# Attention and two MoE layers on one core: the first pass in a computed, pinned order with one PSUM pool, and a second pass that is all Strassen with weight blocks split beforehand

## The chip, the cores and the metric

One core of one Trainium2 chip. The number is the device time of one execution in microseconds; kernels are compared by the median of several runs. All matrix work runs on TensorE (PE; PEld is its weight load), the element-wise work on VectorE (DVE), ScalarE (ACT) and GpSimd (POOL), and SyncE (SP) issues nearly all DMAs.

## The reference

Attention over 4 batches of 8 heads (S = 576, D = 64) with a causal local part and a memory part, then two feed-forward layers over the 2304 tokens (d_model 512):

```
a = softmax(causal(q @ k.T / sqrt(D))); local = a @ v
q_p = elu(q) + 1
mem_out = (q_p @ M_prev) / (q_p . z_prev + 1e-6)
x = g * mem_out + (1 - g) * local            # g = sigmoid(beta), per head
x = (silu(x @ w_gate) * (x @ w_val)) @ w_out # d_ff 1536
h = x @ w_in                                 # d_ff 2048
out = (h * sigmoid(1.702 * h)) @ w_out
```

The weights arrive as float64 and are turned into float32 on the chip.

## The kernel before, in words

**Arithmetic.** A float32 product is made of three matmuls in the fp32r type: each operand is split into a high part (a cast on ACT) and a low part (a subtraction, operand minus high part), and PE sums high x high, low x high and high x low. One matmul is a 128x128 weight block against 288 columns; two of them fill one PSUM tile of two banks (288 + 288 columns, 576 tokens of one batch).

**Weights.** They come in 68 chunks of 128x512: per group of the first layer (3 groups) 8 projection chunks (gate and value) and 4 output chunks, per group of the second layer (4 groups) 4 and 4. The chain of one chunk is: load (SP, tile w), two ACT operations (L140, L141), three on DVE (L144, L146, L147), one add on POOL (L150), which leaves the float32 chunk in a tile wa (three buffers); then the split, hi on ACT (L166) and lo on POOL (L169), into wp (four buffers). Of the 20 pairs of projection chunks POOL also forms four Strassen sums (L178 to L181); these and the chunks themselves go to DRAM as float32. The 28 output chunks go to DRAM split.

**Stages.** (1) The attention of batches 0 and 1 alone: 8 pairs (two heads of one batch each), in an order that `ordered` computes and `pinned` fixes on every engine; it ends with three chunks of weights made. (2) The first pass: both layers for batches 0 and 1 (`moe`: per chunk and batch h, 12 x 2 matmuls, tile m), with the attention of batches 2 and 3 between them: `beside` lists its steps with hand-set costs, and the loop over `moe(xh, xl)` issues them as the pass proceeds, so much attention per half product. The order on an engine is that of the program text. The finished attention goes to DRAM (`stage`). PSUM is split: two tiles for MoE (ps_m) and two for attention (ps_s). (3) The second pass (`second`): both layers for batches 2 and 3. A projection pair is one Strassen unit (`unit`): 7 products of 12 matmuls (tile wb against sums of x, L82) in place of 8, with PSUM results added on DVE into tiles sn; the weight sums are read raw (7 of 128x256 in one load, L730) and split on the spot (ACT L742, POOL L743). The output blocks are plain: 28 chunks x 2 batches x 24 matmuls. The gate is Tanh on ACT with a multiply-add on DVE behind it (L836, L837).

Between the passes, SP loads the attention of batches 2 and 3 back (xr, L966), and `halves` forms the Strassen operands of x: B11, B12, B21, B22 and T1 to T4, each split.

## Time and profile before

| | us |
|---|---|
| median of 3 runs | 1081.33 (1080.96 to 1081.98) |
| profiled execution | 1082.06 |
| its span in the trace | 1080.3 |
| PE busy | 1041.8 (96%) |
| PE's weight load busy | 971.8 (90%) |
| DVE busy | 696.1 (64%) |
| POOL busy | 612.3 (57%) |
| ACT busy | 542.9 (50%) |

Times are read from one profiled execution. An engine is busy while an instruction of it runs; "idle before" a group is the time in which its engine stood still just before, and the arrow names what it waited for. Names such as m, wp, sn are the program's tiles. PEclk is the share of full clock that PE was granted.

### The profile page before, as it was taken

Reading aid. Unit: us, or ns where it says so; the run is one execution under the profiler, and the core shown is the slowest. Engines: PE = TensorE matmul, PEld = TensorE weight load, DVE = VectorE, ACT = ScalarE, POOL = GpSimd, SP = SyncE. Lnnn points to the kernel's source line nnn. Section 1 sums busy time; section 2 is a strip of 40 time slices with the busy share of each in tenths; the row PEclk is TensorE's granted clock in tenths of the full one; section 3 lists DMA queues with packets and bytes.
Section 4 is the critical chain, followed back from the end, with each engine's and each line's share of the span. In section 5 each row is a group of like instructions: output and inputs, shape, how many; then the busy total and the mean of one; then the engine's idle time right before and its main releaser. Section 6 shows DMA issues by size and latency. Waiting matters only on the chain.

```text
span 1080.3 us, 19843 instructions
## 1 busy us (share of the span) xinstructions
PE 1041.8 (96%) x7664; PEld 971.8 (90%) x7664; DVE 696.1 (64%) x1063; ACT 542.9 (50%) x1107; POOL 612.3 (57%) x634
## 2 busy tenths in 40 slices
PE   5989798999999999999999999999999999999998
PEld 2656687899999898989899999999999999999998
DVE  6887589646666777836657448762745778265573
ACT  4887555655545555756556454442513436343230
POOL 6886798866567475665745542661835817153321
PEclk8999999999999999999999999999999999999999
DMA  4332635644454453444434337323222222322102
GB/s 165 114 95 87 216 118 187 219 148 146 151 170 142 132 174 123 157 137 147 161 122 140 115 127 278 110 71 110 70 79 87 85 78 70 112 74 74 59 21 88
DMA packets 46718, 133.93 MB, mean 124 GB/s; under 512 B 7584, under 2 KB 10400, under 8 KB 46624
## 3 DMA queue, kind: packets, MB, share of 16 engines
q1 hardware_dynamic: 46480, 132.67, 36.7%
q8 instruction: 60, 0.98, 0.4%
q14 instruction: 34, 0.28, 0.1%
q10 hardware_dynamic: 144, 0.00, 0.0%
HBM read 92.54 MB, written 40.11 MB: 123 GB/s over the span
## 4 chain that ended last, share of the span: by engine, by line
PE 54%; DVE 3%; ACT 1%; DMA 1%; POOL 1%; issue 1%; SPq 0%; ACTq 0%; DVEq 0%; POOLq 0%
PE m L82 51%; PE o L82 1%; PE s L82 1%; DVE hl L613 1%; PE tp L378 1%; DMA xr<-x 0%; DMA raw<-w 0%; DVE u L683 0%; ACT hh L612 0%; ACT wb L742 0%; POOL wa L150 0%; DVE xl L766 0%; DMA x<-st 0%; DVE wa L147 0%; POOL p L366 0%
## 5 line engine op out<-in xcount | busy, mean ns | idle before, releaser
L82 PE MATMUL m<-hh,wp 128*128 128x288 f32 x1792 | 312.6, 297 | 1.4 <-ACT acc L663 0.7
L82 PEld LDWEIGHTS m<-hh,wp 128*128 128x128 f32 x1792 | 262.2, 189 | 9.5 <-issue 3.2
L82 PE MATMUL m<-xh,wp 128*128 128x288 f32 x1280 | 241.8, 304 | 12.6 <-DVE u L643 8.9
L743 POOL TENSOR_TENSOR wb<-raw,wb 128x256 fp32r<-128x256 f32 x140 | 124.9, 906 | 197.4 <-ACT wb L742 192.3
L82 PEld LDWEIGHTS m<-xh,wp 128*128 128x128 f32 x1280 | 193.9, 191 | 23.8 <-DVE u L643 8.1
L82 PE MATMUL m<-hl,wp 128*128 128x288 f32 x896 | 190.6, 296 | 0.0
L150 POOL TENSOR_TENSOR wa<-wa,wr 128x512 uint32<-128x512 uint32 x68 | 93.6, 1377 | 106.3 <-issue 50.2
L82 PEld LDWEIGHTS m<-hl,wp 128*128 128x128 f32 x896 | 143.6, 188 | 0.4 <-issue 0.4
L82 PE MATMUL m<-xl,wp 128*128 128x288 f32 x640 | 138.2, 298 | 0.0
L82 PE MATMUL m<-xh,wb 128*128 128x288 f32 x640 | 119.0, 296 | 0.0
L169 POOL TENSOR_TENSOR wp<-wa,wp 128x512 fp32r<-128x512 f32 x68 | 92.7, 1364 | 42.5 <-ACT wp L166 42.1
L82 PEld LDWEIGHTS m<-xl,wp 128*128 128x128 f32 x640 | 104.4, 191 | 0.0
L82 PEld LDWEIGHTS m<-xh,wb 128*128 128x128 f32 x640 | 96.9, 189 | 0.0
L742 ACT CAST wb<-raw 128x256 fp32r<-128x256 f32 x140 | 55.6, 404 | 79.1 <-PE m L82 77.6
L366 POOL TENSOR_SCALAR p<-p,sm 128x128 f32<-128x128 f32 (+3 forms) x128 | 75.1, 605 | 28.6 <-DVE sm L357 8.5
L82 PE MATMUL m<-th,wb 128*128 128x288 f32 x480 | 90.3, 296 | 0.0
L144 DVE TENSOR_SCALAR wa<-wa 128x512 f32<-128x512 f32 x68 | 39.3, 578 | 75.6 <-ACT wa L140 75.0
L341 ACT ACTIVATE p<-s,nm 128x128 f32<-128x128 f32 (+3 forms) x128 | 66.0, 528 | 30.5 <-DVE nm L327 29.3
L82 PEld LDWEIGHTS m<-th,wb 128*128 128x128 f32 x480 | 73.2, 189 | 0.0
L140 ACT ACTIVATE wa<-w 128x512 f32<-128x512 f32 x68 | 46.0, 677 | 53.5 <-POOL wp L169 48.9
L613 DVE TENSOR_TENSOR hl<-u,hh 128x576 fp32r<-128x576 f32 x56 | 56.4, 1007 | 25.4 <-ACT hh L612 24.6
L141 ACT ACTIVATE wr<-w 128x512 uint32<-128x512 uint16 x68 | 46.1, 678 | 51.0 <-POOL wa L150 50.4
(136 smaller groups left out, 1830.6 us busy)
## 6 DMA issues: line engine op xcount, KB each, us to landing
w<-w SPq DMA_DIRECT2D x40, 512.0 KB, 3.7
raw<-w SPq DMA_DIRECT2D x20, 896.0 KB, 4.6
w<-wo SPq DMA_DIRECT2D x28, 512.0 KB, 3.6
w<-wp SPq DMA_DIRECT2D x28, 512.0 KB, 2.9
wp<-w SPq DMA_DIRECT2D x28, 512.0 KB, 3.5
w<-sums SPq DMA_DIRECT2D x20, 512.0 KB, 2.8
qk<-qk SPq DMA_DIRECT2D x32, 288.0 KB, 3.7
nq<-nat SPq DMA_DIRECT2D x16, 320.0 KB, 4.1
```

The costliest lines, as they stand in the source:

```text
L82: nc.tensor.matmul(o, w, x, start=start, stop=stop)
L140: nc.scalar.activation(a, top.bitcast(F32), AF.Abs)
L141: nc.scalar.activation(r, rest, AF.Copy, scale=2.0 ** -13)
L144: nc.vector.tensor_scalar(a, a, HIGH, LOW, op0=ALU.min, op1=ALU.max)
L150: nc.gpsimd.tensor_tensor(au, au, r, op=ALU.add)
L169: nc.gpsimd.tensor_sub(wp[:, 1], t, f(wp[:, 0]))
L341: nc.scalar.activation(p[:, j, c:c + n], s[:, j, c:c + n], AF.Exp, bias=nm[:, x, j:j + 1], accum_out=sm[:, x, j:j + 1])
L366: nc.gpsimd.tensor_scalar(p[:, j, c:c + n], p[:, j, c:c + n], sm[:, x, j:j + 1], 1.0, op0=ALU.mult, op1=ALU.mult)
L378: nc.tensor.transpose(t[:, j, c:c + 128], p[:, j, c:c + 128], ident)
L613: nc.vector.tensor_sub(hl, t, f(hh))
L742: nc.scalar.copy(wb[:, 0], src)
L743: nc.gpsimd.tensor_sub(wb[:, 1], src, f(wb[:, 0]))
```

## The change

- **First pass.** `beside`, `alone` and `moe` are replaced by lists of operations: `attend` (attention pairs), `piece` (one weight chunk: load, decode, split, store, sums) and `first_pass` (the MoE products, in halves of 12 matmuls, and what follows them). Each operation has an engine, a cost, a key (when it is due), what it comes after, and what it takes and gives back of counted stocks (buffers). `ordered` runs them through a list schedule, and `pinned` fixes the result on every engine, as for the first stage.
- **PSUM.** One pool of four tiles (psp) serves attention and MoE throughout.
- **Weights in the first pass.** All 34 pairs, output chunks too, get their four sums, and the sums are split at once (ACT cast, DVE subtraction) and stored split. Four chunks, not three, are made at the end of the first stage.
- **Second pass.** Output blocks are Strassen units too: 34 units x 7 products x 12 matmuls. Their right-hand sides are sums of the hidden values (`arrive`: H operands, one buffer each). Blocks are loaded ready split, 256 KB each, 12 ahead. The gates are the Silu and Gelu_apprx_sigmoid tables.
- The first twelve wb blocks of the second pass and the operands of its x are asked for just ahead of the last part (`cut`) of the pinned order.

```
-    ps_m = ctx.enter_context(
-        tc.tile_pool(name="ps_m", bufs=2, space=bass.MemoryType.PSUM, reuse_waits="tile"))
-    ps_s = ctx.enter_context(
-        tc.tile_pool(name="ps_s", bufs=2, space=bass.MemoryType.PSUM, reuse_waits="tile"))
+    psp = ctx.enter_context(tc.tile_pool(name="psp", bufs=4, space=bass.MemoryType.PSUM))
...
-                m = d2.tile([128, 4, 256], F32, tag="sums", name="sums")
-                nc.gpsimd.tensor_add(m[:, 2], a2[:, 0], a2[:, 1])
-                nc.gpsimd.tensor_sub(m[:, 0], m[:, 2], a1[:, 0])
-                nc.gpsimd.tensor_sub(m[:, 1], a1[:, 0], a2[:, 0])
-                nc.gpsimd.tensor_sub(m[:, 3], a1[:, 1], m[:, 0])
-                nc.sync.dma_start(out=kept[i - 1][:, 2:6], in_=m)
...
+        def sum_hi():
+            got["s"] = d2.tile([128, 2, 2, 256], F32R, tag="ms", name="ms")
+            nc.scalar.copy(got["s"][:, :, 0], got["m"].rearrange("p a s n -> p a (s n)"))
+
+        def sum_lo():
+            nc.vector.tensor_sub(
+                got["s"][:, :, 1], got["m"].rearrange("p a s n -> p a (s n)"), f(got["s"][:, :, 0]))
...
+        return [hi, lo, store, sums(2), sum_hi, sum_lo, sum_store(2), sums(4), sum_hi, sum_lo, sum_store(4)]
...
+        op("w", "SP", 0.4, ("big",), (), lambda: load_one(i))
+        op("dec0", "Act", 1.4, ("wr",) + (("wa",) if wide else ()), (), dec(0))
+        op("dec1", "DVE", 2.3, (), (), dec(1))
+        op("dec2", "Pool", 1.45, (), big + ("wr",), dec(2))
+        op("hi", "Act", 0.65, ("wp",), (), spl(0))
+        op("lo", "Pool", 1.4, (), (), spl(1))
...
+            for y, x in enumerate((3, 7)):
+                op(f"sum{y}", "Pool", 1.9, ("m1",) if y == 0 else (), wa * 2 if y else (), spl(x))
+                op(f"shi{y}", "Act", 0.6, ("ms",), (), spl(x + 1))
+                op(f"slo{y}", "DVE", 0.65, (), ("m1",) if y else (), spl(x + 2))
...
+    attend(ops, attb, pairs[2 * HP:], False, stage, lambda t: 8.0 + 15.0 * t, 0.3)
+    for i in range(GIVEN, NCK):
+        piece(ops, i, 7.8 * i - 24.0, ())
+    first_pass(ops, xh, xl, GIVEN)
...
+    order_b, _ = ordered(ops, {
+        "qk": 2, "nq": 2, "zb": 1, "v": 2, "qt": 2, "e": 2, "ph": 2, "s": 1, "m": 1, "mm": 3, "ps": 4, "p": 3, "pt": 1,
+        "big": 3, "wa": 3, "wr": 2, "wp": 4 - GIVEN, "m1": 1, "ms": 2, "u": 3, "hs": 8})
...
+    pinned(ops, order_b[:cut], last)
...
+    ready(12)
+    X = blocks_of_x()
+    pinned(ops, order_b[cut:], last)
...
-        src = load_unit(i)[:, x]
         wb = cb.tile([128, 2, 256], F32R, tag="wb", name="wb")
-        nc.scalar.copy(wb[:, 0], src)
-        nc.gpsimd.tensor_sub(wb[:, 1], src, f(wb[:, 0]))
+        nc.sync.dma_start(out=f(wb), in_=kept[i][:, (0, 1, 3, 4, 2, 5, 6)[x]])
...
+            if half == 0 and (kd, 0, 0) in raw and (kd, 0, 1) in raw:
+                t1 = raw[kd, 0, 0]
+                nc.vector.tensor_sub(t1, raw[kd, 0, 1], t1)
+                two("T1", kd, t1)
+            if all((kd, a, b) in raw for a in range(2) for b in range(2)):
+                t1, b12, b21, b22 = (raw.pop((kd, a, b)) for a in range(2) for b in range(2))
+                nc.vector.tensor_sub(t1, b22, t1)
+                two("T2", kd, t1)
+                (nc.gpsimd if kd == 0 else nc.vector).tensor_sub(b12, b22, b12)
+                two("T3", kd, b12, nc.gpsimd if kd == 0 else nc.vector)
+                nc.gpsimd.tensor_sub(b21, b21, t1)
+                two("T4", kd, b21, nc.gpsimd)
...
+                def outer(d0):
+                    def what(row, h, a, p, again):
+                        d = d0 + row
+                        ac = acc[:, d, h]
+                        if g == 0:
+                            nc.vector.tensor_add(ac, a, p)
+                            return
+                        nc.gpsimd.tensor_add(ac, ac, a)
+                        if layer == 0 or g < n - 1:
+                            nc.vector.tensor_add(ac, ac, p)
+                            return
...
+                run(groups.pop(0), H, [outer(0), outer(2)])
```

PE where the first stage ends (o is the attention's last product, m the MoE's). Before:

```order
L82 MATMUL o<-ph,mz_83 128x288 x2
L82 MATMUL o<-pz_85,v 64x64 x2
L82 MATMUL o<-pt,v 64x192 x2
L82 MATMUL o<-pt,v 64x288 x6
L82 MATMUL o<-pt,v 64x160 x2
L82 MATMUL m<-xh,wp 128x288 x2
L82 MATMUL m<-xl,wp 128x288 x2
```

Now (L90 is the line of `mm` in the new text):

```order
L90 MATMUL o<-ph,mz_89 128x288 x2
L90 MATMUL m<-xh,wp 128x288 x2
L90 MATMUL m<-xl,wp 128x288 x2
L90 MATMUL m<-xh,wp 128x288 x4
L90 MATMUL o<-pz_91,v 64x64 x2
L90 MATMUL o<-pt,v 64x192 x2
L90 MATMUL o<-pt,v 64x288 x6
```

The first 12 matmuls of the first pass now stand ahead of the last o product's main part; before, all of that product came first.

SP between the passes (out: results of batches 0 and 1; xr: attention of batches 2 and 3; raw and wb: weight blocks of the second pass; x2 and x3 are those batches). Before:

```order
L171 DMA w65_131<-wp_7234 128x1024
L730 DMA raw_7693<-w4_88 128x1792
L171 DMA w66_132<-wp_7310 128x1024
L966 DMA xr_7438<-x2_163 128x576
L702 DMA out<-ot_7347 128x576
L966 DMA xr_7440<-x3_164 128x576
L966 DMA xr_7442<-x2_163 128x576
L966 DMA xr_7444<-x3_164 128x576
L966 DMA xr_7466<-x2_163 128x576
```

Now:

```order
L981 DMA xr_7979<-x3_156 128x576
L674 DMA out<-ot_8042 128x576
L753 DMA wb_7945<-w0_92 128x512
L753 DMA wb_7947<-w0_92 128x512
...
L753 DMA wb_7967<-w2_93 128x512
L981 DMA xr_8001<-x2_155 128x576
L981 DMA xr_8003<-x3_156 128x576
L981 DMA xr_8005<-x2_155 128x576
L981 DMA xr_8007<-x3_156 128x576
L674 DMA out<-ot_8070 128x576
```

Twelve wb loads now stand between the sixth out store and the last four xr loads; before, the eight xr loads went between the first out stores, and three raw loads ahead of them all.

POOL in the first pass, one pair of chunks (L150 or L149 is the decode's add, L169 or L165 the low part of the split, L178 to L181 or L187 to L191 the sums, L366 or L412 an attention step). Before:

```order
L150 TENSOR_TENSOR wa_3571<-wa_3571,wr_3572 128x512
L366 TENSOR_SCALAR p_3518<-p_3518,sm_3517 128x512 x2
L178 TENSOR_TENSOR sums_3663<-wa_3571 128x256
L180 TENSOR_TENSOR sums_3663<-wa_3483,wa_3571 128x256
L169 TENSOR_TENSOR wp_3473<-wa_3399,wp_3473 128x512
L179 TENSOR_TENSOR sums_3663<-sums_3663,wa_3483 128x256
L181 TENSOR_TENSOR sums_3663<-wa_3483,sums_3663 128x256
L150 TENSOR_TENSOR wa_3670<-wa_3670,wr_3671 128x512
L169 TENSOR_TENSOR wp_3567<-wa_3483,wp_3567 128x512
```

Now:

```order
L149 TENSOR_TENSOR wa_3997<-wa_3997,wr_3998 128x512
L412 TENSOR_SCALAR p_4019<-p_4019,sm_4018 128x384 x2
L165 TENSOR_TENSOR wp_4081<-wa_3997,wp_4081 128x512
L187 TENSOR_TENSOR sums_4110<-wa_3812 128x256
L188 TENSOR_TENSOR sums_4110<-sums_4110,wa_3997 128x256
L149 TENSOR_TENSOR wa_4026<-wa_4026,wr_4027 128x512
L323 TENSOR_TENSOR nq_2799<-phi_4136,zb_2683 128x640
L190 TENSOR_TENSOR sums_4110<-wa_3997,wa_3812 128x256
L191 TENSOR_TENSOR sums_4110<-wa_3997,sums_4110 128x256
```

The sums of a pair used to go ahead of the split of its second chunk; now they come behind it, in two halves, each followed by a cast and a subtraction on other engines, and the pair's wa tiles are free after the last of them.

## Rows read from the trace of the kernel before

**Rows 1.** Stretches of the span, all engines. Columns: stretch in us and its length, busy us and number of instructions of PE, of its weight load PEld, of DVE, ACT and POOL, then the granted share of PE's clock, the mean busy share of the DMA engines, and GB/s.

```profile
119.00:200.00 81.00, 69.10 (x470) 64.20 (x467) 63.93 (x91) 42.92 (x86) 68.83 (x65) 0.94 0.60 195
132.00:138.00 6.00, 5.25 (x22) 5.26 (x23) 5.71 (x7) 4.31 (x7) 5.72 (x8) 0.50 0.64 250
200.00:660.00 460.00, 457.71 (x3395) 426.58 (x3394) 286.52 (x456) 250.48 (x484) 275.53 (x271) 1.00 0.44 150
300.00:400.00 100.00, 99.96 (x751) 93.06 (x750) 65.51 (x105) 52.31 (x104) 62.80 (x62) 1.00 0.48 158
656.00:664.00 8.00, 8.00 (x63) 8.00 (x62) 6.13 (x9) 4.03 (x7) 0.00 (x0) 1.00 1.02 366
680.00:1070.00 390.00, 390.00 (x2929) 389.99 (x2928) 235.44 (x295) 148.03 (x288) 178.54 (x168) 1.00 0.23 79
900.00:1000.00 100.00, 100.00 (x753) 100.00 (x753) 56.68 (x68) 42.03 (x82) 41.23 (x40) 1.00 0.24 80
```

**Rows 2.** The same view for tile m alone, the MoE matmuls and what reads their results. Columns as in rows 1.

```profile
119.00:200.00 81.00, 60.66 (x406) 58.42 (x407) 11.40 (x16) 5.11 (x8) 0.00 (x0) 0.94 0.60 195
200.00:660.00 460.00, 389.14 (x2763) 370.12 (x2762) 74.48 (x100) 41.24 (x64) 0.00 (x0) 1.00 0.44 150
300.00:400.00 100.00, 83.50 (x593) 79.22 (x592) 17.91 (x24) 5.19 (x8) 0.00 (x0) 1.00 0.48 158
660.00:680.00 20.00, 19.45 (x146) 19.17 (x145) 3.81 (x6) 0.63 (x1) 0.00 (x0) 1.00 0.58 208
```

**Rows 3.** First PE's waits from 119 to 200 us (waiting group, releaser: us in total, times, longest), then rows of PE's timeline (start us, us, engine, line, operation, out<-in, shapes, count, idle before and its releaser): the first matmuls of the first pass, those behind the longest of the waits, and the first of the second pass.

```profile
PE m L82 <- DVE u L643: 8.9, 4, 4.2
PE m L82 <- DVE u L652: 2.4, 2, 1.4
...
119.69 0.53 PE L82 MATMUL m<-xh,wp 128*128 128x288 f32 x2
...
132.75 0.85 PE L82 MATMUL m<-xh,wp 128*128 128x288 f32 x2 [4.24 <-DVE u L643]
...
660.38 0.43 PE L82 MATMUL m<-xh,wb 128*128 128x288 f32 x2
```

**Rows 4.** Groups of instructions of the first pass by line and shape, on POOL, ACT and DVE: out<-in, count, busy us, mean ns of one, idle before and its releaser. The first two are the shortest and the longest of the four sums.

```profile
L178 POOL TENSOR_TENSOR sums<-wa 128x256 f32<-128x256 f32 x20 | 15.9, 794 | 0.5
L179 POOL TENSOR_TENSOR sums<-sums,wa 128x256 f32<-128x256 f32 x20 | 17.1, 855 | 0.1
L150 POOL TENSOR_TENSOR wa<-wa,wr 128x512 uint32<-128x512 uint32 x68 | 93.6, 1377 | 106.3 <-issue 50.2 <-DVE wa L147 44.8 <-DVE sm L357 4.3
L169 POOL TENSOR_TENSOR wp<-wa,wp 128x512 fp32r<-128x512 f32 x68 | 92.7, 1364 | 42.5 <-ACT wp L166 42.1
...
L140 ACT ACTIVATE wa<-w 128x512 f32<-128x512 f32 x68 | 46.0, 677 | 53.5 <-POOL wp L169 48.9 <-POOL sums L181 3.8 <-DMA w<-wa 0.6
L166 ACT CAST wp<-wa 128x512 fp32r<-128x512 f32 x68 | 41.8, 616 | 20.5 <-PE m L82 19.0 <-POOL wa L150 1.4
...
L147 DVE SCALAR_TENSOR_TENSOR wa<-w,wa 128x512 uint32<-128x512 uint32 x68 | 57.9, 851 | 1.2
L613 DVE TENSOR_TENSOR hl<-u,hh 128x576 fp32r<-128x576 f32 x56 | 56.4, 1007 | 25.4 <-ACT hh L612 24.6
L146 DVE TENSOR_SCALAR wa<-wa 128x512 uint32<-128x512 uint32 x68 | 42.2, 621 | 1.7
L144 DVE TENSOR_SCALAR wa<-wa 128x512 f32<-128x512 f32 x68 | 39.3, 578 | 75.6 <-ACT wa L140 75.0
```

**Rows 5.** A row of SP's timeline near the end of the first pass, the issue of one DMA. Columns as in the timeline of rows 3.

```profile
652.17 0.38 SPq L966 DMA_DIRECT2D xr<-x  x1
```

**Rows 6.** Groups of instructions by line and shape of the second pass (L766: the operands of x), on DVE, POOL and ACT. Columns as in rows 4.

```profile
L845 DVE SCALAR_TENSOR_TENSOR hl<-sn,hh 128x576 fp32r<-128x576 f32 x24 | 24.4, 1018 | 6.2 <-ACT hh L843 6.1
L847 DVE TENSOR_TENSOR hl<-u,hh 128x576 fp32r<-128x576 f32 x16 | 19.4, 1212 | 1.6 <-ACT hh L843 0.6
L818 DVE TENSOR_TENSOR sn<-sn,m 128x576 f32<-128x576 f32 x20 | 15.0, 751 | 9.4 <-PE m L82 9.3
L766 DVE TENSOR_TENSOR xl<-xr,xh 128x576 fp32r<-128x576 f32 x6 | 4.5, 755 | 1.6 <-ACT xh L765 1.6
...
L862 POOL TENSOR_TENSOR sn<-sn,u 128x576 f32<-128x576 f32 x24 | 38.7, 1613 | 8.6 <-DVE u L837 7.6 <-DVE sn L827 1.0
...
L913 ACT ACT_TABLE_LOAD x1 | 1.3, 1283 | 1.2 <-PEq L1025 1.2
```

**Rows 7.** DMA issues of the page, the two kinds of stores of results: out<-in, engine, operation, count, KB each, median us from issue to landing.

```profile
out<-ot SPq DMA_DIRECT2D x15, 288.0 KB, 2.6
...
out<-ot SPq DMA_DIRECT2D x2, 144.0 KB, 1.7
```

**Rows 8.** Rows of the timelines of ACT and POOL for the decode of two pairs of chunks in the first pass, the first and the last step of each, and one POOL step of the attention in between. Columns as in the timeline of rows 3.

```profile
450.81 0.66 ACT L140 ACTIVATE wa<-w 128x512 f32<-128x512 f32 x1
...
455.45 2.19 POOL L366 TENSOR_SCALAR p<-p,sm 128x128 f32<-128x128 f32 x4
...
461.58 0.98 POOL L181 TENSOR_TENSOR sums<-wa,sums 128x256 f32<-128x256 f32 x1
...
466.83 0.67 ACT L140 ACTIVATE wa<-w 128x512 f32<-128x512 f32 x1 [0.57 <-POOL wp L169]
...
473.96 0.75 POOL L181 TENSOR_TENSOR sums<-wa,sums 128x256 f32<-128x256 f32 x1
```

More of the change, by code (lines that the diff above doesn't have):

```diff
@@ L1 @@
+import bisect
+import heapq
 from contextlib import ExitStack
@@ L185, in split_stages, with store @@
-        return one, two
-    def ahead(i):
-        upto("load", i + 6, load_one)
-        upto("split", i + 3, split_one)
-        upto("dec", i + 4, dec_one)
-    def next_w():
-        i = state["use"]
-        state["use"] += 1
-        ahead(i)
-        return parts.pop(i)
+        def store():
+            for r in (1,) if row[i] else (0, 1):
+                for w in range(2):
+                    nc.sync.dma_start(
+                        out=k[:, 6 if row[i] else r, w].rearrange("p (s n) -> p s n", s=2),
+                        in_=two_halves(i, f(wp[:, w]))[:, r])
@@ L473, in ordered, with free @@
+    LAG = {"SP": 2.5}
+    SIGNAL = 0.2
     def ordered(ops, stock):
         stock = dict(stock)
-        left, end, order = dict(ops), {}, []
-        busy, times, now = {}, [0.0], 0.0
-        while left:
+        need, then, at = {}, {}, {}
+        lists, order, running, now = {}, [], [], 0.0
+        def free(n, t):
+            bisect.insort(lists.setdefault(ops[n][0], []), (ops[n][2], str(n), n, t))
+        for n, o in ops.items():
+            need[n] = len(set(o[3]))
+            at[n] = 0.0
+            for x in set(o[3]):
+                then.setdefault(x, []).append(n)
+        for n in ops:
+            if not need[n]:
+                free(n, 0.0)
+        busy, events = {}, [0.0]
+        while len(order) < len(ops):
+            now = heapq.heappop(events)
@@ L499, in ordered @@
-            times = sorted({t for t in times if t > now})
-            assert times or not left, sorted(left)
-            now = times[0] if times else now
-        return order, now
-    LAG = {"SP": 2.0}
-    def pinned(ops, order):
-        last = {}
+            engines = {ops[n][0] for n in busy}
+            again = True
+            while again:
+                again = False
+                for e, ready in lists.items():
+                    if e in engines:
+                        continue
+                    for y, (key, _, n, t) in enumerate(ready):
+                        if t <= now and all(stock[x] > 0 for x in ops[n][4]):
+                            break
+                    else:
+                        continue
+                    ready.pop(y)
+                    for x in ops[n][4]:
+                        stock[x] -= 1
+                    engines.add(e)
+                    order.append(n)
+                    done = now + ops[n][1]
+                    busy[n] = done
+                    heapq.heappush(events, done)
+                    for m in then.get(n, ()):
+                        need[m] -= 1
+                        lag = LAG.get(e, SIGNAL) if ops[m][0] != e else 0.0
+                        at[m] = max(at[m], done + lag)
+                        heapq.heappush(events, at[m])
+                        if not need[m]:
+                            free(m, at[m])
+                    again = True
+                    break
@@ L724, in tile_attention_moe_moe @@
-    got = {"make": 0, "use": 0}
-    blocks, units = {}, {}
-    def load_unit(i):
-        if i not in units:
-            units[i] = cw.tile([128, 7, 256], F32, tag="raw", name="raw")
-            nc.sync.dma_start(out=units[i], in_=kept[i])
-        return units[i]
+    groups = []
+    for g in range(3):
+        groups += [(12 * g + 2 * k,) for k in range(4)] + [(12 * g + 8, 12 * g + 10)]
+    for g in range(4):
+        p = 36 + 8 * g
+        groups += [(p, p + 2)] if g == 0 else [(p,), (p + 2,)]
+        groups.append((p + 4, p + 6))
@@ new lines, in second, with hidden @@
+                        run(groups.pop(0), X, [hidden])
+                else:
+                    def hidden(kd):
+                        def what(row, h, a, p, again):
+                            c = total(a, p, again)
+                            nc.scalar.activation(c, c, AF.Gelu_apprx_sigmoid)
+                            arrive(kd, row, h, c)
+                        return what
+                    if g == 0:
+                        run(groups.pop(0), X, [hidden(0), hidden(1)])
+                    else:
+                        for kd in range(2):
+                            run(groups.pop(0), X, [hidden(kd)])
```

688 lines of the change are left out of this document (306 added, 382 removed).

## Prediction, written before the changed kernel was run

> **What bounds the kernel now.** I read the stages first, then the matmuls alone, then what ended the waits, then the price of single operations. In [rows 1] the reader is to see two regimes: from 680 us to 1070 us (the second pass) PE and its weight loads are busy without a gap, while DVE is busy 60% and POOL 46% of the stretch; before that (the first pass) PE is full from 200 us on, with DVE 62%, POOL 60% and ACT 54%, but in 119 to 200 us PE is busy 69 of 81 us at a mean clock share of 0.94, and POOL and DVE are at 85% and 79%. So PE bounds nearly all of it, and the only stretch with a hole is the start of the first pass.
>
> The price of one MoE matmul (tile m): 753 in 100 us of the second pass, 132.8 ns [rows 1, 2]. With it the first pass can be split. From 200 to 660 us it issues 2763 m matmuls, 366.9 us, and 3395 - 2763 = 632 of the attention. In 300 to 400 us there are 593 of the one (78.8 us) and 751 - 593 = 158 of the other in the remaining 21.2 us: 134 ns each [rows 1, 2]. At that price the 632 take 84.7 us, so 460 - 366.9 - 84.7 = 8.4 us are lost there. The same sum for 119 to 200 us: 406 m, 53.9 us, 64 others, 8.6 us, 18.5 us lost. Most of that is PE waiting on DVE, 8.9 us and 2.4 us behind two DVE groups [rows 3]; after one such wait, of 4.24 us, the clock granted from 132 to 138 us is 0.50, 1.2 GHz, and two matmuls take 0.85 us where they took 0.53 us at 119.7 us [rows 1, 3]. So the first pass gives away 27 us, two thirds of it in its first 81 us.
>
> **The sum, part by part**, against the profiled execution (1082.06 us, span 1080.3; the median of the runs is 0.73 us lower).
>
> *Fewer matmuls in the second pass.* Before: 20 hidden units x 7 products x 12 matmuls and 28 output blocks x 2 halves x 24, 1680 + 1344 = 3024. After: 34 units x 7 x 12 = 2856. 168 x 132.8 ns = **-22.3 us**, all on PE, which sets the time there. Nothing else of the second pass shortens it.
>
> *First pass, work added beside PE.* Every pair of weight chunks, not 20 of 34, now gets its four sums: 14 x 4 POOL operations at 0.79 to 0.86 us, 46 us. The sums are split as well: 68 ACT casts of 128x512 at 616 ns, 42 us, and 68 DVE subtractions of 128x512, nearest row hl 128x576 at 1007 ns, by size 895 ns, 61 us [rows 4]. Spread over the 541 us of the first pass (119.7 to 660.4 us, from its first matmul to the first with wb [rows 3]) that is 8, 8 and 11 points: POOL 68%, ACT 62%, DVE 74%. All stay below PE, so hidden as far as the order lets them; I take +2 us. Where they are not hidden, see the slower rival: up to +38 us. The stores grow to some 10 issues per pair on SP (six of wp, two of ms, two loads) at 0.38 us each [rows 5], about 4 us of the 15.9 us that a pair takes: hidden.
>
> *First pass, order.* In the new order PE takes the first 12 m matmuls ahead of the last o product, four chunks instead of three are split before the pass begins, and attention and MoE share four PSUM tiles instead of two and two. It advances 7.9 chunks per attention pair all the way (8.0, 15.5, 23.5, ... 63.0 chunks at the eight o products), where the order before rushed 14 chunks ahead of the first and squeezed the last. That rush is what loaded DVE and POOL in 119 to 200 us. Bounds: all 27 us come back, or none. The four-chunk start removes the first DVE wait but the added sums and splits fall into the same stretch, so I take half of the 18.5: **-9 us**. First pass together -7 (from -27 to +38).
>
> *First stage.* The same 8 pairs. POOL gets two pairs' sums (8 operations, 6.6 us) near its end, but PE no longer waits for the last pair to begin the pass. 0 (-2 to +4).
>
> *Between the passes.* In the new SP order twelve wb loads stand ahead of the four xr loads that hold the second half of x. From the last hidden product PE has eight output products, 192 x 132.8 ns = 25.5 us. The first wb load follows an out store that needs the sixth of them, so it is issued at 19.1 + 1 = 20 us; 12 x 256 KB at the 366 GB/s that 656 to 664 us shows [rows 1] take 8.6 us, and the next x rows land near 30 us; with an ACT cast (616 ns for 512 columns, so some 0.69 us for 576) and a DVE subtraction (0.755 us) behind them [rows 4, 6] it is 31.5 us. PE has four half products (PSUM holds four), 3.2 us, to bridge 25.5 to 28.7. **+3 us** (0 to 8); the boundary before lost 0.6 us in 660 to 680 (146 x 0.1328 of 20 us) [rows 2].
>
> *Second pass, DVE.* The output products now need Strassen operands of the hidden values. In a group of the second layer DVE has, beside two hidden units (14 products x 12 x 132.8 ns = 22.3 us of PE), 14 PSUM adds at 751 ns and 16 operations between SBUF tiles. Those take 755 ns where POOL is still and 1018 to 1212 ns beside it [rows 6]. 10.5 + 16 x 1.0 = 26.5 us, above the 22.3 us; the following 14 output products leave DVE idle half the time and take the rest. What is late next is T2 and T3: their low parts must be ready 7.5 and 9.1 us after the last hidden product. At 1.0 us each it just fits, at 1.2 us it is late by 1 to 2 us. I take 0.7 us in each of seven groups, **+5 us** (0 to 18). The row shows a DVE operation with two SBUF inputs stretched by 0.25 to 0.46 us where POOL works. The Trainium skill (SBUF — State Buffer, Who interferes with whom) has it that such a DVE instruction and a GpSimd instruction that reads SBUF exclude each other for their whole length, and here POOL gets eight more additions per output group; by that rule the upper price of 1.2 us is the likelier and the term would be 13 us, not 5. The trace agrees in direction, not in full length: the mean is nearer 1.0 than 0.755 plus a POOL operation of 1.6 us.
>
> *Small ones.* Two more ACT_TABLE_LOADs at 1283 ns stand on ACT, busy 38% of the second pass [rows 1, 6]: 0. Silu and Gelu take the place of Tanh on the same shape, and the DVE operation that followed a Tanh goes: the count of DVE above is without it. wb loads come split, so 140 ACT casts and 140 POOL subtractions go; 238 x 256 KB in some 385 us is 162 GB/s, under half of the 366 GB/s shown: 0. The last store is one of 288 KB (2.6 us) where now it is a half (1.7 us) [rows 7], and the add before it is whole as well: **+1**.
>
> Sum: -22.3 - 7 + 3 + 5 + 1 = -20.3. 1082.1 - 20.3 = 1061.8 profiled, **1061 us** as median of the runs.
>
> **Rivals.** *(A) The first pass reaches its floor:* the whole 27 us but 2 come back. For it: one computed order for all five engines, chunk and attention in step. Against: DVE at 74%. -22.3 - 25 + 2 + 3 + 5 + 1 = -36 : 1045 us. Weight loads are busy 92.7% of 200 to 660 us and 100% of 680 to 1070 us [rows 1]. The Trainium skill (Perfetto Trace Analysis, Identifying the Most-Contended Engine) judges PE's room by that share, not by matmul time; as an estimate by it 33 us are free in 200 to 660 us alone and (A) would end near 1020 us. The m loads explain 366.9 of their 370 us, so the rest of the share is attention, and I keep to (A).
>
> *(B) Slower: the ring of three wa tiles paces the first pass.* A pair's two wa tiles are now given back only after its last sum, and every sum waits for the split, which was not so: before, the sums went ahead of the split, and 28 chunks had none. From one release to the next the third tile's successor must pass ACT 1.36 (two operations of 0.68), DVE 2.05 (three), POOL 1.38, ACT 0.62, POOL 1.36, 1.65, ACT 0.62, DVE 0.8, POOL 1.65 = 11.5 us [rows 4] and nine handovers. Before, a pair took 541/34 = 15.9 us. The other terms sum to -13.3 (without the first pass), so the pass may grow to 554 us; with two pairs given and some 9 us behind the last, 32 pairs may take 17.0 us each, handovers of 0.61 us. The trace has both sides: one chunk went from its ACT start at 450.81 us to its pair's last sum at 462.56, 11.75 us for 8.1 us of work and three handovers (1.2 each); the next pair's from 466.83 to 474.71, 7.9 us, no handover to be seen [rows 8]. At 0.7 a pair takes 17.8 us and the pass 32 x 17.8 + 9 = 579: 37.6 - 13.3 = 24 us slower, 1106 us. Against it: in the slow case POOL did an attention step of 2.19 us [rows 8] and another chunk's split in between, and by the new keys a late chunk goes ahead of both; and PE's order keeps step with the attention, where a PE short of chunks would have run ahead with it.
>
> *(C) DVE bounds the second pass:* the two-input operations at 1212 ns throughout [rows 6], each group of the second layer 3 us late, of the first 2: 18 us instead of 5, 1074 us.
>
> *(D) The change does not do what it says:* its order shows 2856 matmuls with wb and no weight cast in the second pass; no chance given.
>
> **How the numbers follow.** Forecast 0.60 (its own range 1050 to 1069), (A) 0.15, (C) 0.17, (B) 0.08. The range 1043 to 1076 leaves out (B), the far part of (A) and of (C). A measurement of this kernel tells about 0.2%, 2.2 us, from no change. Faster by more: all but (B) and a little of (C), but a mild (B) is still faster: 0.91; within: 0.02; slower: 0.07.
>
> **What would show it.** Right: 680 us and on, 753 matmuls per 100 us still, and 168 fewer of them; the first pass with fewer DVE waits in its first 80 us; DVE near 80% in the second pass; gaps of PE under 2 us, on hb tiles behind DVE, at the start of each output group; one gap of some 3 us on xh behind xr. Wrong: PE waiting on wp behind POOL or ACT throughout the first pass (B), PE waiting on hb for over 2 us in every group (C), or a first pass under 522 us (A).

## The result, and the profile after

The changed kernel takes 1088.12 us (median of 5 runs, 1085.41 to 1089.70), the kernel before 1081.69 us in the same comparison: ratio 1.0055, 95% interval 1.0039 to 1.0072. It is **slower by 6.4 us**, where 20 us less were forecast. The profiled execution is the fastest of its five, 1085.41 us with a span of 1083.6; it is 3.35 us above the profiled one of before, and the ledger below adds up to about that.

By stretches of the span (columns as in [rows 1]), all engines:

```profile
119.00:200.00 81.00, 70.69 (x504) 64.05 (x502) 64.61 (x86) 44.22 (x85) 59.76 (x58) 0.94 0.66 215
200.00:660.00 460.00, 455.47 (x3393) 426.21 (x3390) 365.34 (x524) 276.55 (x539) 326.74 (x317) 1.00 0.60 199
660.00:692.00 32.00, 24.86 (x166) 23.84 (x165) 20.92 (x31) 10.18 (x16) 1.43 (x2) 0.89 0.84 292
900.00:1000.00 100.00, 97.38 (x717) 95.53 (x717) 78.58 (x103) 38.99 (x61) 32.04 (x21) 1.00 0.57 158
```

and tile m alone, as in [rows 2]:

```profile
119.00:200.00 81.00, 57.37 (x384) 54.83 (x384) 11.87 (x16) 5.18 (x8) 0.00 (x0) 0.94 0.66 215
200.00:660.00 460.00, 387.30 (x2787) 373.73 (x2788) 73.47 (x100) 41.74 (x64) 0.00 (x0) 1.00 0.60 199
```

Three things are to be seen. The main part of the first pass is as it was: 2787 m at 132.8 ns and 606 others at 134 ns make 451.3 of 460 us, 8.7 us lost, where the same sum gave 8.4 before. It is so although DVE went from 62% to 79% and POOL from 60% to 71%. The first 81 us lost 13.9 us by that sum (384 m, 120 others), where it was 18.5. And the second pass is no longer full: 717 matmuls in 900 to 1000 us, where it was 753 [rows 1].

PE's waits from 660 us on show where (waiting tile, releaser: us in total, times, longest):

```profile
PE m L90 <- ACT xh L772: 6.4, 1, 6.4
PE m L90 <- DVE hbl L838: 4.8, 7, 1.0
PE m L90 <- ACT sn L816: 1.1, 1, 1.1
PE m L90 <- DVE tl L773: 1.1, 2, 0.6
PE m L90 <- DVE sn L825: 0.8, 3, 0.3
PE m L90 <- DMA wb<-w: 0.7, 1, 0.7
```

xh is the operand of x at the boundary of the passes, hbl the low part of a hidden sum, and the tl and the first sn wait are at the boundary of the two layers. Here a wait costs more than its length: the waits listed come to 14.9 us, and behind a wait the next matmul starts stand further apart (0.21 us behind the one on wb, 0.40 us behind the one on xh, where 0.133 is usual). So I summed what the intervals between successive matmul starts have beyond 0.133 us: from the last matmul of the first pass (672.29 us) to the end it is 25.4 us, **10.2** at the boundary of the passes (672 to 689 us), **10.0** at the start of six of the seven output groups (0 in the first, 1.2 to 1.9 in each of the others) and **5.1** at the boundary of the layers (893 to 905 us). Before, the boundary of the passes lost 0.9 us so counted, and the rest of the second pass nothing.

**The boundary of the passes.** SP, ACT and PE (timelines; start, us, engine, line, operation, idle before and its releaser):

```profile
669.53 5.88 SPq L753 DMA_DIRECT2D wb<-w  x12
676.62 0.32 SPq L981 DMA_DIRECT2D xr<-x  x1
...
682.39 0.67 ACT L772 CAST xh<-xr 128x576 fp32r<-128x576 f32 x1 [7.86 <-DMA xr<-x]
...
683.11 0.85 PE L90 MATMUL m<-xh,wb 128*128 128x288 f32 x2 [6.36 <-ACT xh L772]
```

Twelve issues, one in 0.49 us, stand on SP between the first pass's sixth out store and the x rows; the first x operand of the second half is cast 12.9 us after the first wb issue. The issues were over after 5.9 us, the transfers were not. The stretch between the first landing and the cast, and the times from issue to landing of the twelve wb loads and of the four xr loads behind them:

```profile
672.60:682.40 9.80, 3.42 (x24) 3.22 (x24) 3.89 (x6) 1.27 (x3) 0.00 (x0) 0.92 1.03 379
...
DMA to landing us min/median/max: 3.1/5.5/6.8
...
DMA to landing us min/median/max: 5.7/5.8/5.9
```

The first block landed 3.1 us after its issue; from then on the DMA engines were busy throughout (1.03) at 379 GB/s, and the x rows landed behind the blocks, 5.7 us or more after their own issue. So the x rows waited for the bytes ahead of them. Behind the gap two matmuls take 0.85 us, as they did behind the long wait in [rows 3]: PE's granted clock is 0.50, 1.2 GHz, in 683.1 to 687.1 us, and 0.89 on the mean in 660 to 692 us.

**An output group.** DVE, then ACT and POOL, where the last hidden unit of a second-layer group ends:

```profile
1010.62 0.76 DVE L853 TENSOR_TENSOR sn<-sn 128x576 f32<-128x576 f32 x1
1011.41 1.88 DVE L859 TENSOR_TENSOR sn<-sn 128x576 f32<-128x576 f32 x1
1013.21 1.99 DVE L838 TENSOR_TENSOR hbl<-sn,hbh 128x576 fp32r<-128x576 f32 x1
1015.23 0.76 DVE L857 TENSOR_TENSOR sn<-sn 128x576 f32<-128x576 f32 x1
1015.91 0.75 DVE L838 TENSOR_TENSOR hbl<-sn,hbh 128x576 fp32r<-128x576 f32 x1
...
1016.03 0.67 ACT L837 CAST hbh<-sn 128x576 fp32r<-128x576 f32 x1 [2.03 <-DVE sn L857]
...
1011.19 3.39 POOL L904 TENSOR_TENSOR acc<-acc,sn 128x576 f32<-128x576 f32 x2 [3.27 <-ACT sn L816]
```

Two of DVE's operations take 1.88 and 1.99 us, while POOL adds two blocks to acc; their neighbours take 0.75. The low part in the row at 1015.91 is what PE waits for from 1015.7 to 1016.7 us. By the source it is T3's (its difference is L859): T2's high part is cast only at 1016.03, behind L857, so T2's low part comes later still.

**The start of the first pass.** ACT and PE:

```profile
126.76 0.65 ACT L630 ACTIVATE u<-m 128x576 f32<-128x576 f32 x1
133.18 0.74 ACT L311 ACTIVATE phi<-nq 128x640 f32<-128x640 f32 x1 [5.77 <-DMA nq<-nat]
...
138.28 0.62 ACT L196 CAST ms<-sums 128x512 fp32r<-128x512 f32 x1 [3.08 <-POOL sums L191]
...
141.46 0.63 ACT L630 ACTIVATE u<-m 128x576 f32<-128x576 f32 x1
...
143.02 0.82 PE L90 MATMUL m<-xh,wp 128*128 128x288 f32 x2 [5.12 <-DVE u L634]
```

The second Tanh stands on ACT behind the attention's first two steps on nq, which wait for loads, and behind the cast of a sum. That sum is late for the same reason: its POOL step had waited 4.5 us for DVE, and DVE for ACT's step on nq. PE stops for 5.1 us and starts again at a granted clock of 0.50 (in 143 to 148 us; 0.82 us for two matmuls).

### The profile page after: what moved, and what is told of

Read it like the earlier page. It is cut to its first block, busy times and chain, and to the rows that moved or that the text cites. A ratio compares the mean times of both kernels' runs of the same rounds, so it can differ in the third digit from the quotient of the medians.

```text
span 1083.6 us, 20483 instructions
## 1 busy us (share of the span) xinstructions
PE 1024.3 (95%) x7496; PEld 947.6 (87%) x7496; DVE 838.0 (77%) x1210; ACT 555.8 (51%) x1077; POOL 636.2 (59%) x610
## 4 chain that ended last, share of the span: by engine, by line
PE 66%; DVE 18%; DMA 4%; ACT 4%; issue 4%; POOL 3%; SPq 1%; POOLq 0%; DVEq 0%; ACTq 0%
PE m L90 55%; PE o L90 5%; PE s L90 3%; PE tp L424 2%; DVE hbl L838 2%; DVE hl L646 1%; DVE sn L832 1%; DMA w<-ms 1%; ACT p L387 1%; DMA nq<-nat 1%; DMA w<-w 1%; POOL acc L904 1%; DVE sn L859 1%; DVE wa L143 1%; DVE ms L199 1%
## 5 line engine op out<-in xcount | busy, mean ns | idle before, releaser
L90 PE MATMUL m<-xh,wp 128*128 128x288 f32 x1280 | 237.8, 302 | 6.8 <-DVE u L634 5.7
L90 PEld LDWEIGHTS m<-xh,wp 128*128 128x128 f32 x1280 | 193.1, 191 | 14.8 <-issue 8.7
L90 PE MATMUL m<-hh,wp 128*128 128x288 f32 x896 | 157.6, 298 | 0.0
L149 POOL TENSOR_TENSOR wa<-wa,wr 128x512 uint32<-128x512 uint32 x68 | 95.8, 1409 | 79.9 <-DVE wa L146 42.0
L90 PE MATMUL m<-hbh,wb 128*128 128x288 f32 x784 | 138.3, 297 | 0.8 <-DVE sn L825 0.8
L90 PE MATMUL m<-xl,wp 128*128 128x288 f32 x640 | 138.3, 298 | 0.0
L90 PEld LDWEIGHTS m<-hh,wp 128*128 128x128 f32 x896 | 131.2, 189 | 6.7 <-issue 2.6
L90 PE MATMUL m<-xh,wb 128*128 128x288 f32 x640 | 120.8, 299 | 7.2 <-ACT xh L772 6.4
L90 PEld LDWEIGHTS m<-hbh,wb 128*128 128x128 f32 x784 | 116.0, 188 | 1.9 <-DVE sn L825 1.5
L165 POOL TENSOR_TENSOR wp<-wa,wp 128x512 fp32r<-128x512 f32 x68 | 95.0, 1397 | 27.0 <-ACT wp L162 23.5
L90 PEld LDWEIGHTS m<-xh,wb 128*128 128x128 f32 x640 | 98.1, 191 | 8.0 <-ACT xh L772 6.6
L90 PEld LDWEIGHTS m<-xl,wp 128*128 128x128 f32 x640 | 104.4, 191 | 0.2 <-DVE xl L671 0.2
L837 ACT CAST hbh<-sn 128x576 fp32r<-128x576 f32 x98 | 64.8, 673 | 63.4 <-DVE sn L857 18.2
L90 PE MATMUL m<-hl,wp 128*128 128x288 f32 x448 | 96.0, 296 | 0.0
L412 POOL TENSOR_SCALAR p<-p,sm 128x128 f32<-128x128 f32 (+3 forms) x128 | 81.6, 655 | 18.3 <-DVE sm L404 9.4
L90 PE MATMUL m<-th,wb 128*128 128x288 f32 x480 | 90.7, 296 | 1.7 <-ACT sn L816 1.1
L90 PE MATMUL m<-hbl,wb 128*128 128x288 f32 x392 | 84.9, 299 | 5.3 <-DVE hbl L838 4.8
L904 POOL TENSOR_TENSOR acc<-acc,sn 128x576 f32<-128x576 f32 x40 | 59.7, 1504 | 49.2 <-ACT sn L816 27.4
L838 DVE TENSOR_TENSOR hbl<-sn,hbh 128x576 fp32r<-128x576 f32 x77 | 72.6, 954 | 18.4 <-ACT hbh L837 17.5
L879 POOL TENSOR_TENSOR sn<-sn 128x576 f32<-128x576 f32 x18 | 25.4, 1434 | 98.0 <-ACT sn L874 98.0
L832 DVE TENSOR_TENSOR sn<-sn,m 128x576 f32<-128x576 f32 x80 | 59.4, 750 | 28.8 <-PE m L90 28.0
```

The source lines that it names most:

```text
L90: nc.tensor.matmul(o, w, x, start=start, stop=stop)
L149: nc.gpsimd.tensor_tensor(au, au, r, op=ALU.add)
L165: nc.gpsimd.tensor_sub(wp[:, 1], t, f(wp[:, 0]))
L412: nc.gpsimd.tensor_scalar(p[:, j, c:c + n], p[:, j, c:c + n], sm[:, x, j:j + 1], 1.0, op0=ALU.mult, op1=ALU.mult)
L832: nc.vector.tensor_add(c, a, p)
L837: nc.scalar.copy(hi, src)
```

## The experiments

All are edits of the changed kernel unless said; "less" is against its 1088.1 us.

**1. x operands first.**

```
-    ready(12)
     X = blocks_of_x()
+    ready(12)
```

> Changed kernel with the x operands asked for ahead of the twelve wb loads: on SP ten of the twelve now stand behind the last four xr loads. Theory Q (SP's queue made the gap at 676.45 us): those loads go out some 6 us earlier, the gap of 6.5 us falls below 1 us and the 2.4 us of half clock behind it go; 7 to 9 us less than the changed kernel. Rival R (the transfers of 650 to 690 us are bound by bandwidth, 279 GB/s in that stretch): the xr loads come earlier but the first wb blocks later by as much, PE waits on wb in its place; 0 to 2 us less.

Measured 1084.84 us, 3.3 less. The wait of 6.4 us became two of 1.0 and 1.2 us (PE behind ACT xh still), and the loss at the boundary by the sum of intervals fell from 10.2 to 6.1 us. SP's order made the gap, as Q says, but only 4 of the 10 us go with it, not the 7 to 9 that Q expected: behind the mended order PE still waits for the x rows' own chain (load, cast, subtraction), which begins as late as the sixth out store, and the x rows still land 4.7 us or more after their issue.

**2. Without POOL's first addition.**

```
-                        nc.gpsimd.tensor_add(ac, ac, a)
+                        if (row, h) != (0, 0):
+                            nc.gpsimd.tensor_add(ac, ac, a)
```

> Changed kernel without POOL's first addition to acc of each output unit (the one for row 0, h 0; the shares of earlier groups are left out of those blocks of the result). DVE's instructions are the same in kind and number. Theory X (a DVE operation with two SBUF inputs and a POOL operation hold each other up): the two DVE operations that took 1.88 and 1.99 us at 1011.4 and 1013.2 us take 0.75, T2's low part is ready 2.3 us earlier, the PE gap of 1.0 to 1.3 us per group goes in six groups; 6 to 9 us less than the changed kernel. Rival L (DVE has too many operations in a hidden group, whoever runs beside it): durations and gaps stay; under 2 us less.

Measured 1081.72 us, 6.4 less. DVE at the same place as above:

```profile
1007.76 0.76 DVE L853 TENSOR_TENSOR sn<-sn 128x576 f32<-128x576 f32 x1
1008.55 0.76 DVE L859 TENSOR_TENSOR sn<-sn 128x576 f32<-128x576 f32 x1
1009.26 0.76 DVE L838 TENSOR_TENSOR hbl<-sn,hbh 128x576 fp32r<-128x576 f32 x1
1010.05 0.76 DVE L857 TENSOR_TENSOR sn<-sn 128x576 f32<-128x576 f32 x1
```

The same operations take 0.76 us each, and the loss in the output groups fell from 10.0 to 3.0 us. It was the collision, not DVE's number of operations: theory X holds, L falls.

**3. Plain output blocks.**

```
-                run(groups.pop(0), H, [outer(0), outer(2)])
+                plain(groups.pop(0), held_h)
```

> Changed kernel with plain output blocks in the second pass, as before: 28 blocks of 2 x 24 matmuls on four weight blocks per unit (in the place of the lower left block, which is not stored, another of the same size is used), hidden values split once, no sums of them. 168 matmuls more, 22.3 us. If the waits on hb tiles (10 us) and at the layer boundary (5 us) and the longer tail (1 us) all come from the Strassen outputs, these go: 22.3 - 16 = 6 us more than the changed kernel. If they come from elsewhere (loads of wb, the gates), they stay: 22 us more.

Measured 1095.97 us, 7.9 more. From 692 us on PE waits once, 0.3 us. So the 168 matmuls bring 22.3 us and the Strassen outputs cost some 14 of them (22.3 - 7.9): the waits on hb and at the boundary of the layers both belong to the outputs.

**4. No sums in the first pass, 5. only the old ones.** In 4 `sums`, `sum_hi` and `sum_lo` are left out of every pair; in 5 the sums of the 20 projection pairs are kept, without a split.

> Changed kernel without the weight sums of the first pass and without their splits (in their place the split chunk is stored, so the second pass works on other weights of the same size): 112 us less on POOL, 42 on ACT, 58 on DVE, loads and stores the same. Theory W (the added element-wise work eats what the computed order gives): the first pass and the end of the first stage shrink by 10 us or more, to near their floor. Theory D (late loads and the order make the stalls, such as the one at 137.6 us behind ACT's wait on nq): the stalls stay, under 4 us less than the changed kernel.

> Changed kernel with the sums of the 20 projection pairs only, as in the kernel before, and no split of any (in place of the split sums the split chunk is stored, so the second pass works on other weights of the same size). Against the changed kernel that takes 46 us of POOL, 42 of ACT and 58 of DVE out of the first pass, what the prediction put at 2 us; against the kernel without any sums it puts 65 us of POOL back. If the added work costs what I now think, 8 us or more less than the changed kernel (1080 us or less); if it was hidden, within 3 us of it, and the 14.5 us that the kernel without sums gained came from the 20 pairs' sums.

Measured 1073.63 us (14.5 less) and 1080.49 us (7.6 less). The 14.5 us are what W expected (10 or more), not D (under 4). What the change adds to the first pass costs 7.6 us, not 2. The profiled executions of 5 and of the changed kernel are 4.8 us apart, and 4.4 of them lie at the boundary of the passes: the loss from 640 us on is 21.1 us in 5 where it is 25.5. In 5 the last x loads go out at 645 us, not at 679, and PE does not wait for xh; it waits twice for low parts of hidden values, 3.9 us in all. The boundary's loads are pinned behind the last step of the weights, so the last pair's sums and splits can delay them; that these alone did it is not shown, since the computed order changed too. Where the other 3 us of the medians lie the traces do not show: the wait at the start of the pass is still there in 5 (6.0 us).

**6. Loads planned later everywhere, 7. attention loads planned later.**

```
-    LAG = {"SP": 2.5}
+    LAG = {"SP": 5.0}
```

```
+    ops["late"] = "late", 10.0, -100.0, (), (), (), lambda: None
+    for n in [n for n in ops if n[0] in ("load_qk", "load_nq", "load_v")]:
+        e, us, key, after, takes, gives, do = ops[n]
+        ops[n] = e, us, key, after + ("late",), takes, gives, do
```

> Changed kernel with the planner told that a load lands 5.0 us after its issue, not 2.5 (the trace has 3.0 to 4.6 us for 288 to 512 KB); both computed orders change, the operations do not. Theory D (loads that come later than planned stall what is pinned behind them, all through the first pass): 4 to 8 us less than the changed kernel. Rival S (only the start of the pass is wrong, since the first attention loads wait for tiles that the first stage still holds, and the rest runs to plan): the gap at 137 us stays, within 3 us of the changed kernel.

> Changed kernel with one entry more in the planner: no load of the first pass's attention before 10 us of the plan. In the trace the first nq load is issued at 126.8 us, when the first stage's tiles come free, and lands at 133.2 us, 14 us after the pass began; the plan had it land at 2.9 us, and the Tanh of the second product stood behind it on ACT. Theory S: ACT does not stand before the first Tanhs, the gap of 5.4 us at 137.6 us and the half clock behind it (2 us) go; 4 to 8 us less than the changed kernel. Rival W (sums and splits fill POOL and DVE there): PE waits as long, on wp or on the sums' engines; under 2 us less.

Measured 1087.32 us for 6, no change within the spread of the runs, with a wait of 7.4 us at the start of the pass (D falls, S holds), and 1084.71 us for 7, 3.4 less: between what S and W expected. In 7 the Tanhs run, but a wait of 4.9 us remains at 139 us, now in front of the attention's first scores. Its stretches:

```profile
119.00:200.00 81.00, 74.72 (x548) 68.39 (x548) 69.59 (x95) 45.40 (x93) 61.60 (x60) 0.95 0.63 205
200.00:660.00 460.00, 452.08 (x3370) 422.80 (x3370) 356.27 (x517) 275.42 (x531) 324.73 (x316) 1.00 0.60 199
```

The first 81 us issue 44 matmuls more than the changed kernel's 504, nearly 6 us of PE, as S expected; the next 460 us issue 23 fewer than its 3393, 3 us. The new computed order gives back behind the seam half of what it gains there.

**8. Three edits together.** Experiments 1 and 7, and in place of leaving the addition out:

```
-                        nc.gpsimd.tensor_add(ac, ac, a)
+                        if (row, h) != (0, 0):
+                            nc.gpsimd.tensor_add(ac, ac, a)
                         if layer == 0 or g < n - 1:
                             nc.vector.tensor_add(ac, ac, p)
+                            if (row, h) == (0, 0):
+                                nc.vector.tensor_add(ac, ac, a)
```

> Changed kernel with three edits: x operands asked for ahead of the wb loads (3.3 us less by itself), the first addition to acc of each output unit on DVE behind the PSUM addition instead of on POOL (leaving it out gave 6.4 us), and the attention loads of the first pass planned 10 us later (4 to 8 us by theory S, under 2 by theory W). All of the result is computed. Sum of the three: 1088.1 - 3.3 - 5.5 - 6 = 1073 us by theory S, 1079 us by theory W; the two DVE operations added per group should lie in DVE's idle half of the output group.

Measured 1074.39 us, ratio to the kernel before 0.9932 (0.9920 to 0.9945). The three add up: by themselves they gave 3.3, 3.4 and (experiment 9) 5.7 us, 12.4 together, and here 13.7. Its remaining gap at the start of the pass (ACT, SP, PE):

```profile
137.66 0.62 ACT L196 CAST ms<-sums 128x512 fp32r<-128x512 f32 x1 [3.08 <-DMA w<-ms]
...
129.41 4.08 SPq L170 DMA_DIRECT2D w<-wp  x4
134.70 1.29 SPq L295 DMA_DIRECT2D mz<-mem  x2
136.32 0.33 SPq L203 DMA_DIRECT2D w<-ms  x1
...
144.52 1.65 PE L90 MATMUL s<-qk 64*128 64x128 f32 x8 [4.64 <-POOL qk L302]
```

The cast of a sum waits for an ms tile, whose store stands on SP behind four stores of wp and two loads of the attention; the attention's own step on POOL (qk) is pinned behind the split. So the added sums and the late loads meet in one queue.

**9. The addition on DVE alone.** The edit shown in 8, without the two others.

> Changed kernel with the first addition to acc of each output unit on DVE behind the PSUM addition instead of on POOL, nothing else. By theory X the waits on T2 go as they did where the addition was left out (6.4 us), and the two DVE operations of 0.75 us per group fall into DVE's idle time of the output products: 5 to 6.5 us less than the changed kernel. If DVE has no room there, 3 us or less.

Measured 1082.44 us, 5.7 less.

**10. POOL helps DVE at the boundary of the layers**, on top of 8:

```
+            eng = nc.gpsimd if pool and kd == 0 else nc.vector
-            nc.vector.tensor_sub(b12, b22, b12)
-            two("T3", kd, b12)
+            eng.tensor_sub(b12, b22, b12)
+            two("T3", kd, b12, eng)
...
+            eng.tensor_sub(b21, b21, t2)
+            two("T4", kd, b21, eng)
```

> The kernel with three edits, and at the boundary of the two layers four of DVE's operations on the operands of x (T3 and T4 of the first half: two differences, two low parts) on POOL, which is idle there. In the changed kernel PE lost 5.1 us there behind DVE. Theory X (DVE and POOL hold each other up where both read SBUF alone): POOL's four take 1.4 us each and stop DVE for as long, 5.7 us against 3.0 us saved; the loss at the boundary grows to 6 to 8 us, the kernel is 1 to 3 us slower than the one with three edits. Rival L (only DVE's number of operations counts): the loss falls to 2 to 3 us; 2 to 3 us faster.

Measured 1077.14 us, 2.7 slower than 8. POOL, then DVE, of its timeline:

```profile
883.47 2.01 POOL L785 TENSOR_TENSOR acc<-acc 128x576 f32<-128x576 f32 x1 [2.03 <-DVE acc L908]
885.45 1.91 POOL L789 TENSOR_TENSOR acc<-acc,t 128x576 f32<-128x576 f32 x1
887.32 3.78 POOL L773 TENSOR_TENSOR tl<-acc,th 128x576 fp32r<-128x576 f32 x2
...
884.10 2.00 DVE L779 TENSOR_TENSOR t<-acc 128x576 f32<-128x576 f32 x1
886.02 1.95 DVE L773 TENSOR_TENSOR xl<-acc,xh 128x576 fp32r<-128x576 f32 x1
887.89 1.95 DVE L782 TENSOR_TENSOR t<-acc,t 128x576 f32<-128x576 f32 x1
889.77 1.95 DVE L773 TENSOR_TENSOR tl<-t,th 128x576 fp32r<-128x576 f32 x1
891.64 0.74 DVE L785 TENSOR_TENSOR acc<-acc 128x576 f32<-128x576 f32 x1
```

Four operations of POOL and four of DVE take turns, 1.9 to 2.0 us each; as soon as POOL is done DVE is back at 0.74. The loss at the boundary of the layers is 8.0 us where it is 5.2 in 8. Four operations fewer on DVE made its chain longer: X again, and with the opposite sign of edit.

**11. The attention loads planned for 16 us, 12. for 22 us**, on top of 8 (10.0 becomes 16.0, 22.0).

> The kernel with three edits, and the attention loads of the first pass planned for 16 us, not 10. With 10 us the gap near 138 us stayed (4.9 us, PE's s waiting for qk on POOL, behind a split that waits for ACT, behind a store of ms in SP's queue). Theory S (the seam: the second plan starts with idle engines and free buffers where the first one still runs): PE has more products to do before it needs attention, the gap falls under 2 us; 2 to 4 us faster than the kernel with three edits. Rival W (splits and stores of the weights stall the start whatever the attention does): the gap moves to wp; within 1 us.

> The kernel with three edits, and the attention loads of the first pass planned for 22 us (10 us gave 1074.4, 16 us 1068.6). Theory S (what counts is that the attention is not asked for before its tiles and loads are there, about 14 us into the pass): at 16 us that is met, 22 us gives the same within 2 us, 1066.5 to 1070.5, the start of the pass without a gap over 2.5 us. Rival O (each computed order is a draw, and the one at 16 us a good one): any value from 1066 to 1076 us, with gaps elsewhere in the pass.

Measured 1068.56 us (ratio to before 0.9895, 0.9876 to 0.9913) and 1070.30 us (0.9897, 0.9881 to 0.9914). Like 8, these two beat both kernels. Stretches of 8, then of 11:

```profile
119.00:200.00 81.00, 74.85 (x545) 68.24 (x544) 68.78 (x94) 45.80 (x94) 62.12 (x61) 0.94 0.62 207
200.00:660.00 460.00, 451.99 (x3358) 422.71 (x3358) 357.00 (x517) 275.75 (x531) 324.92 (x315) 1.00 0.60 198
```

```profile
119.00:200.00 81.00, 74.61 (x548) 68.08 (x547) 67.17 (x95) 45.43 (x94) 60.71 (x60) 0.97 0.61 206
200.00:660.00 460.00, 455.30 (x3393) 427.07 (x3392) 362.52 (x518) 275.48 (x532) 327.05 (x317) 1.00 0.60 201
```

In the first 81 us both issue some 40 matmuls more than the changed kernel (504), over 5 us of PE: that is the seam. The difference between them lies behind it: 3358 against 3393 from 200 us on, 35 matmuls or 4.7 us. The changed kernel has 3393 there too, so 11 does not gain there; 8 had lost it. So S holds for the start, and O has a share too: the computed order of the rest is worth several us from one setting to the next. S is not met in full: 11 is 5.8 us faster than 8, where 2 to 4 were expected, and while the wait on qk falls to 1.6 us, another of 3.1 us stands at 155 us; in 12 one of 3.8 us at 161 us remains, more than S allowed.

## Why the prediction was wrong, step by step

| step | predicted | profiled execution |
|---|---|---|
| fewer matmuls, second pass | -22.3 | -22.3 |
| first stage | 0 | +2.3 |
| first pass | -7 | -3 |
| between the passes | +3 | +9.3 |
| DVE in the output groups | +5 | +10.0 |
| boundary of the layers | not in the sum | +5.1 |
| last store | +1 | +2.1 |
| sum | -20.3 | +3.5, measured +3.35 |

The largest term came out. What failed are the terms for the seams, where PE goes over from one pass, layer or group to the next: between the passes, in the output groups and at the boundary of the layers they were put at +8 (3, 5 and nothing) and measured +24.4. The rest is mostly the first pass, which gave 3 us and not 7, with the added work put at +2 that costs 7.6 (4.4 of them at the boundary of the passes), and the first stage, put at 0.

- *Fewer matmuls.* Right: 2856 of them, 753 per 100 us wherever PE does not wait, and experiment 3 puts them back at that price.
- *First stage.* The first m starts at 119.10 us where it was 119.69, but the last o product's main part now lies behind the first 16 matmuls of the pass: 32 matmuls that run in 16 pairs side by side, from 122.44 to 125.36 us, 2.9 us. PE stops for 5.4 us at 111 us, behind a POOL step of the attention that has sums of the first pair ahead of it; before, its last wait there was 1.7 us. The sums explain little of it: in experiment 4, without any, the same wait takes 4.6 us. What else makes it was not tried.
- *First pass.* From its first m to its last it takes 553.3 us. Without the o product that moved in (2.9 us) and the last 96 of its m matmuls (12.8 us), which stood behind the first wb matmul before, that is 537.6 us where it was 540.7: 3 us less, where I took 7. The sum at 134 ns flatters the first 81 us (4.6 us less lost), since 70 of their 120 other matmuls are of o, where it was 8 of 64, and in pairs these take some 91 ns each. What failed is the reason given ("the four-chunk start removes the first DVE wait"): it did, and a new wait came in its place, since the second plan starts with idle engines and free buffers while the first attention load can only go out at 126 us. The planner had it land at 2.9 us of the pass. Experiment 7 shows it by the first 81 us, and 8, 11 and 12 keep that gain.
- *The added work* ("hidden as far as the order lets them; I take +2") was 7.6 us by experiment 5. The shares of DVE and POOL said that there was room, and there was, in 200 to 660 us. As far as the traces show it, the price was paid at the boundary of the passes, where the x operands go out later.
- *Between the passes.* The mechanism was named (twelve wb loads ahead of four xr loads), the size was not. The bandwidth held (366 GB/s taken, 379 measured), but the term had the x rows land some 10 us after the first wb issue and no time for the first block to land (3.1 us); the cast came 12.9 us after that issue, and what the granted clock of 0.50 behind the gap cost (2.4 us) was not in the term. The bound of 8 was too low as well. Experiment 1 takes 4 of the 10 us away.
- *DVE.* Rival (C) had the mechanism and 18 us; I took 5, it was 10.0. "At 1.0 us each it just fits" went wrong because an average was spread over all operations: most take 0.75 us, and the two that meet POOL ahead of T3's low part take 1.9 to 2.0. The Trainium skill (SBUF — State Buffer, Who interferes with whom) states that a DVE instruction with two SBUF inputs contends with a GpSimd instruction that reads SBUF, by an exclusive lock, and that one with at most one SBUF input, outside the 2-port perf modes, does not. Experiments 2 and 10 agree with the first: 0.76 us without POOL beside it, 1.95 with it, a little under the 2.18 us that one operation of each in turn would take (0.75 + 1.43). The changed kernel's trace agrees with the second: the additions that read PSUM (L832, 750 ns on the mean, 80 of them) are not stretched, and 59 additions of that kind that had POOL's two-input operations beside them for nine tenths of their length or more took 748 ns. By that rule the prediction had 13 us; it was nearer than mine.
- *Boundary of the layers.* It was missing. Plain output blocks end one by one, so the next layer's operands were formed along the way; of two Strassen units run side by side six of the eight results come in the last ten products and the last three in the last three, and some twenty DVE operations of 0.75 us follow them. Without Strassen outputs (experiment 3) no wait is left there.
- *Last store.* DVE's last addition waits 0.79 us for POOL's addition to acc, a term that I did not have.
- *Rival (B)*, the ring of wa tiles, did not come: no wait on a chunk of weights is among PE's long ones, and 200 to 660 us lost 8.7 us where it was 8.4. The slower side came from elsewhere, from seams rather than from a resource.

What stays open: the boundary of the passes still loses 6.0 us in experiment 11, the layers' 5.2; what makes the first stage's wait of 5.4 us; where 3 of the 7.6 us of the added work go; and how much of the spread between computed orders is luck.

## What to carry to other kernels

A change that trades PE time for element-wise work is decided at the seams, not by the shares of busy time: list for every boundary (stage, pass, layer, group) which results now come last together, what chain follows them, and what is queued ahead of that chain on SP. A pinned order is as good as its starting state: one computed as if engines and buffers were free at its start pays at the first load. And a POOL operation beside a DVE chain on SBUF operands stretches that chain, here by 1.2 us for each, so moving work from DVE to an idle POOL can slow it (experiment 10), and moving it to a busy DVE can help (experiment 9).

## What the runs showed of the hardware

- DVE additions of two SBUF tiles of 128x576 take 0.75 us alone and 1.88 to 2.00 us while POOL works on SBUF tiles; POOL's own take 1.43 us alone and 1.9 us in such a row. Both lose. Additions with one operand in PSUM take 0.75 us either way.
- A wait of 6.4 us of PE was followed by matmuls of 0.85 us for two, at a granted clock of 0.50 (1.2 GHz) in 683.1 to 687.1 us; the wait cost 8.9 us in all (6.5 + 2.4).
- On SP twelve wb loads of 256 KB were issued in 5.88 us, 0.49 us each, and landed 3.1 to 6.8 us after their issues, at 379 GB/s; a load behind them landed 5.7 us after its own. Here the bytes ahead, not the issues, set when it landed.
